# Spare matmuls and a new order in the boot of an RWKV-6 and tanh-shrink kernel

## The chip, the cores and the metric

The kernel runs on one core of one Trainium2 chip. The metric is the device time of one execution in microseconds (us). The engines are named as the profile names them: PE (matmuls), PEld (its weight loads), DVE (elementwise work), ACT (activations and copies), POOL, and SP, which mostly issues transfers.

## The reference

Two stages follow each other. The first is a recurrence over time for each of 4 batches and 8 heads; the second takes the result as 3072 rows of 384 columns.

```python
B, H, S, D = 4, 8, 768, 48
for t in range(S):
    cur = np.einsum('bhd,bhe->bhde', u[None] * kt, vt)
    y[:, :, t] = np.einsum('bhd,bhde->bhe', rt, state + cur)
    state = wt[:, :, :, None] * state + np.einsum('bhd,bhe->bhde', kt, vt)
# x: y as (3072, 384)
h = x @ w_in            # 384 -> 2048
g = h - np.tanh(h)
out = g @ w_out         # 2048 -> 384
```

## The kernel before, in words

**Blocks and tiles.** The work is cut into eight blocks, one for each batch and half of the sequence (384 tokens). A block needs its attention result `xT` (three tiles of 128 rows x 384 tokens), and then runs 16 tiles f0 to f15 of the second stage. In tile f, PE forms `hp` from `xT` and `w_in` (L703, six instructions), ACT moves it out as `h` (L706), DVE and ACT form `g` by a polynomial (`s`, `qa`, and the two products of L709), and two tiles later PE adds `g` times `w_out` into the three `acc` banks (L780). `hp` has one buffer, so hp of f+1 waits for h of f. From block 2 on a scheme with fewer products takes the place of L780.

**Attention.** The eight heads are four pairs; a half is two pairs (`HALVES`: pairs 2,3 first, then 0,1). A half has these steps, with a block's six chunks of 64 tokens:

- `behind` (a scan on DVE over the decays, with a small memset on POOL), `take_whole`, `before` (reciprocal and scan on DVE);
- `times_behind`, `times_before` (products with k and r on DVE), `times_u` (k scaled on ACT);
- `turn` (transposes on PE, copied to `ks` by ACT), `own` and `earlier` (scores within a chunk on PE, L434, put into the tile `scores` through a mask by DVE, L441);
- `update_1` (key-value products on PE, L482) and `update_2` (the states of the chunks, ten steps on DVE for block 0, L494 to L504);
- `from_scores` (L562) and `from_states` (L545), which add into two PSUM tiles `yp`, one for even and one for odd pairs; `result_out` copies them to `xT` and to `late` (pair 3), and `fill_holes` spreads `late` over the free rows of `xT` by six small transfers.

The two kinds of result matmuls are kept apart by a drain of PE and a wait on a semaphore (L578, L583), unless `more` says that the same kind goes on.

**The order.** PE, SP, DVE and ACT carry out their instructions in the order in which the code issues them. Block 0's attention is written out by hand in `boot` (L912), with nothing of the second stage to run beside it. For the others `plan(i)` (L869) says in which tile of the running block which step is issued: `phases` (steps with PE work) and `before` for the next block, `ahead` for the one after next, `loads` for transfers. A step's DVE part is issued behind that tile's own DVE operations.

**The weights.** They come as 64-bit numbers and are converted in the kernel: three ACT instructions (L249, L252, L253) and then two on DVE (L256, L257) for each tile f. `raw` has five buffers. Three loads are issued at the start; tiles 0 to 2 are converted in `boot`, tiles 3 to 15 in block 0's tiles. There the ACT part of conversion f+3 is issued in tile f and its DVE part in tile f+1, after s of f+1; so DVE's part of conversion 11 follows s of f9, and hp of f11 needs it.

**Scratch.** `boot` has four PSUM tiles of two banks in rotation (`scratch`); a new use waits for the last reader of the old one.

Of the kernel before, what the change touches and what calls it, by code (L numbers as in the profile page):

```python
# [41 lines left out]
BF16 = mybir.dt.bfloat16  # L42
# [8 lines left out]
B, H, S, D = 4, 8, 768, 48  # L51
P = 128
# [11 lines left out]
ALL = tuple(range(NPAIR))  # L64
# [55 lines left out]
def kernel(  # L120
# [12 lines left out]
    nc = tc.nc  # L133
# [26 lines left out]
    start = const.tile([P, UP * NCH * LP], F32, name="start", tag="start")  # L160
# [31 lines left out]
    ident = const.tile([P, P], F32, name="ident", tag="ident")  # L192
# [50 lines left out]
    def convert(f, raw, _, halves=False):  # L243


        lo, hi = raw[:, :, 0], raw[:, :, 1]
        a = w_sb[:, f, :].bitcast(I32)
        up = conv.tile([P, 2 * DM], I32, name="up", tag="up", bufs=4)
        nc.scalar.activation(out=a.bitcast(F32), in_=hi.bitcast(F32), func=AF.Copy, scale=HIGH_SCALE)  # L249
        low, high = (up.bitcast(t).rearrange("p (n two) -> p n two", two=2)[:, :, i]  # L250
                     for i, t in enumerate((U16, F16)))
        nc.scalar.activation(out=high, in_=hi.bitcast(F32), func=AF.Copy, scale=SIGN_SCALE)  # L252
        nc.scalar.activation(out=low, in_=lo.bitcast(U32), func=AF.Copy, scale=2.0 ** -29)  # L253

        def part(at):
            return [lambda: nc.vector.tensor_single_scalar(a[:, at], a[:, at], 3, op=ALU.logical_shift_left),  # L256
                    lambda: nc.vector.tensor_tensor(out=a[:, at], in0=a[:, at], in1=up[:, at], op=ALU.add)]  # L257

        if halves:
            return part(slice(0, DM)), part(slice(DM, 2 * DM))  # L260
        return part(slice(0, 2 * DM))

    def scratch(ps):
        return ps.tile([P, 2, BANK], F32, name="att", tag="att")

    fence, fences = tc.alloc_semaphore("fence"), []

    class Block:
# [177 lines left out]
        def own(self, ps, p0):  # L446
            return self.masked(ps, "k", "r", masks["diagonal"], p0)

        def earlier(self, ps, p0):
            return self.masked(ps, "post", "pre", masks["above"], p0)  # L450
# [132 lines left out]
                nc.tensor.drain().then_inc(fence, 1)  # L583
                fences.append(None)

        def result_out(self, pairs, apart=False, engines=(nc.scalar.copy,)):
            copies = []
            for p in reversed(pairs):
                n = p // 2
                src = self.yp[p % 2][:, :, n * NCP * L:(n + 1) * NCP * L].rearrange("e a (c t) -> e c a t", t=L)  # L590
                dst = self.xT[p] if p < KC else self.late
                dst = dst.rearrange("e (c a t) -> e c a t", a=2, t=L)
                for rows in (slice(0, D), slice(64, 64 + D)) if apart else (slice(0, P),):
                    copies.append(engines[p % len(engines)](out=dst[rows], in_=src[rows]))
            return copies[0]

        def fill_holes(self, engines):
# [102 lines left out]
    def first(xT, f, ps):  # L700
        hp = ps.tile([P, NB], F32, name="hp", tag="hp")
        for kc in reversed(range(KC)):
            nc.tensor.matmul(hp, lhsT=w_in_sb[:, f, kc, :], rhs=xT[kc],  # L703
                             start=(kc == KC - 1), stop=(kc == 0))
        h = dense.tile([P, NB], F32, name="h", tag="h")
        return h, nc.scalar.activation(out=h, in_=hp, func=AF.Copy, scale=1.0 / UPSCALE)  # L706
# [162 lines left out]
    def plan(i):  # L869


        converted = ()
        if i == 0:
            phases = {4: "turn", 6: "update", 8: "own", 11: "earlier", 13: "result 1"}
            before = {0: ("behind 0", "take_whole 0"), 1: ("times_behind 2",), 2: ("times_behind 0",),
                      3: ("before 2",), 4: ("times_u 2",), 5: ("before 0", "times_u 0"), 8: ("times_before", "held")}
            ahead = {14: ("behind 2", "take_whole 2"), 15: ("behind 0", "take_whole 0")}
            converted = range(READY, NF)
            loads = {f: "weights" for f in (0, 1, 3, 4, 5, 6, 7, 8, 9, 10)}
            loads.update({2: "v", 11: "w", 12: "k", 13: "r"})  # L880
        else:
            phases = {4: "earlier", 7: "turn", 10: "update", 12: "result 1"}
            if i == 1:
                before = {0: ("before 2",), 1: ("before 0",), 2: ("times_behind 2", "times_behind 0"),
                          3: ("times_before", "held")}
            else:
                before = {0: ("times_behind 2",), 1: ("times_behind 0",), 3: ("times_before", "held")}
            before.update({4: ("bound 2",), 5: ("product_u",), 6: ("bound 0", "product_r"), 7: ("product_sum",),
                           8: ("diagonal_in 2",), 9: ("diagonal_in 0",)})
            ahead = {10: ("behind 2", "take_whole 2"), 12: ("behind 0", "take_whole 0"), 13: ("before 2",),  # L890
                     15: ("before 0",)}
            loads = {1: "v", 3: "tokens k", 4: "tokens r", 7: "w", 9: "k", 11: "r"}
        return phases, before, ahead, converted, loads

    READY = 3
# [3 lines left out]
    raws = []  # L899
# [12 lines left out]
    def boot(ps, blk, later):  # L912
        h1, h2 = HALVES
        for p0 in HALVES:
            for name in ("w", "k", "r"):
                blk.load(name, p0, UP)
        blk.load_v()
        for _ in range(3):
            more_weights(nc.sync)
        ready = []  # L920

        def converted():
            for op in ready.pop(0):
                op()

        both = (h1, h1 + 1), (h2, h2 + 1)
        blk.behind(h1, UP)
        blk.take_whole(h1, UP)
        blk.before(h1, UP)
        blk.times_behind(h1, UP)  # L930
        blk.times_u(h1, UP)
        blk.turn(ps, h1)
        own = blk.own(ps, h1)
        blk.times_before(h1, UP)
        earlier = blk.earlier(ps, h1)
        blk.bound(h1)
        blk.bound(h2)
        blk.behind(h2, UP)
        blk.take_whole(h2, UP)
        blk.times_behind(h2, UP)  # L940
        blk.times_u(h2, UP)
        blk.turn(ps, h2)
        ins = blk.before(h2, UP)
        begin_behind(ins, later.load("w"))
        own()
        own = blk.own(ps, h2)
        blk.times_before(h2, UP)
        earlier()
        blk.update_1(ps)
        own()  # L950
        ready.append(convert(*raws.pop(0), halves=True))
        blk.results(ps)
        blk.result("from_scores", both[0])
        blk.update_2()
        ready.append(convert(*raws.pop(0)))
        later.bound(h1)
        blk.result("from_states", ALL, cs=(0, 1), more=True)
        earlier = blk.earlier(ps, h2)
        blk.result("from_states", ALL, cs=(2,))
        earlier()  # L960
        blk.result_out(both[0], True)
        later.bound(h2)
        blk.fill_holes([nc.sync, nc.scalar, nc.gpsimd])
        more_weights(nc.sync)
        blk.result("from_scores", both[1], True)
        for op in ready[0][0]:
            op()
        ins = blk.result_out(both[1], True, (nc.scalar.copy, nc.vector.tensor_copy))
        begin_behind(ins, more_weights(nc.sync))
        more_weights(nc.sync)  # L970
        later.load("k")
        later.load("r")
        nc.sync.dma_start(out=u_row, in_=u_all)
        blk.held(0, NPAIR)
        ready[0] = ready[0][1]
        converted()
        ready.append(convert(*raws.pop(0)))
        converted()
        later.prepare("behind 2")
        later.prepare("take_whole 2")  # L980
        converted()

    with tc.tile_pool(name="ps_boot", bufs=4, space=PSUM) as ps_boot:
        xT = blocks[0].begin()
# [4 lines left out]
    acc = [ps_d.tile([P, BANK], F32, name=f"acc{j}", tag=f"acc{j}") for j in range(NB // P)]  # L989
    count = const.tile([P, 1], F32, name="count", tag="count")  # L990
    ahead_of_h, rest, formed, extra, behind, due, summed = [], [], [], [], [], [], []
# [14 lines left out]
    for i, blk in enumerate(blocks):  # L1006
        here = xT
        later = blocks[i + 1] if i + 1 < len(blocks) else None
# [9 lines left out]
        phases, before, ahead, converted, loads = plan(i)  # L1018
# [3 lines left out]
        for f in range(NF):  # L1022
            now = i * NF + f
            for op in ahead_of_h:
                op()
            h, made = first(here, f, ps_d)
            g, ahead_of_h, square, later_ops = slight(h, now, i, f)
            for op in rest + behind + square + formed + extra:
                op()
            rest, behind, formed = later_ops, [], []  # L1030
# [41 lines left out]
            name, ins = loads.get(f), None  # L1072
            if name == "weights":
                ins = more_weights(nc.sync)
            elif name and name.startswith("tokens"):
                ins = later.load_tokens(name[-1]) if later else None
            elif name == "v":
                ins = later.load_v() if later else None
            elif name and after:
                ins = after.load(name)  # L1080
# [92 lines left out]
```

## Time and profile before

| what | value |
|---|---|
| median of 3 runs | 576.61 us (574.99 to 576.81) |
| profiled execution | 577.62 us |
| its span, first to last instruction | 575.8 us |
| busy in the span: PE, PEld, DVE, ACT, POOL | 552.6, 404.0, 486.9, 345.1, 10.9 us |
| mean granted clock of PE | 0.987 |
| hp of f0, f1, f2 of block 0 start | 28.70, 33.54, 38.33 us |
| hp of f11 of block 0 starts | 79.23 us |
| block 1's first hp starts | 104.02 us |

Each row of a timeline has its start in us from the start of the span, its length, the engine, the line of the kernel, the operation, what it writes and reads, the shape and the count. In brackets stands how long the engine had been idle before it, and what ended that idle time; "issue" means that the profile shows nothing that it waited for. In the page's slices each digit is a fortieth of the span (14.4 us) and the busy share in tenths; the row PEclk is the clock that PE was granted, in tenths of full speed.

### The profile page before, as it was taken

How to read it: one execution, taken by the hardware profiler on the slowest of the kernel's cores; microseconds unless marked ns; L12 is line 12 of the kernel's file. 1: busy time of each engine (PE TensorE's matmuls, PEld its weight loads, DVE VectorE, ACT ScalarE, POOL GpSimd, SP SyncE). 2: the span in 40 equal slices, each digit the busy share in tenths (PEclk: the TensorE clock that was granted, in tenths of full speed). 3: DMA queues.
4: the chain of work that ended last, by engine and by line, in shares of the span. 5: the costliest groups of instructions: out<-in, count | busy, mean ns of one | idle time of the engine just before them, and what ended most of it. 6: DMA issues, size and time to landing. Idle time of an engine off the chain costs nothing.

```text
span 575.8 us, 13873 instructions
## 1 busy us (share of the span) xinstructions
PE 552.6 (96%) x5644; PEld 404.0 (70%) x5644; DVE 486.9 (85%) x944; ACT 345.1 (60%) x702; POOL 10.9 (2%) x39
## 2 busy tenths in 40 slices
PE   3699999999999999999999999999999999999996
PEld 3546656566665787877877787778878777777763
DVE  8889996888879998889899988989998998668673
ACT  4889875333236765677565784667555775667441
POOL 6000000000000000000000000000000000000000
PEclk9869999999999999999999999999999999999999
DMA  8495553231302231032122222122321400100101
GB/s 313 133 390 188 173 176 121 72 95 57 111 12 84 83 111 59 10 95 87 56 67 83 84 85 84 52 61 76 102 62 47 125 1 3 40 14 1 43 1 44
DMA packets 32452, 50.38 MB, mean 88 GB/s; under 512 B 2560, under 2 KB 30336, under 8 KB 32384
## 3 DMA queue, kind: packets, MB, share of 16 engines
q1 hardware_dynamic: 32112, 49.36, 26.9%
q8 instruction: 45, 0.74, 0.5%
q14 instruction: 23, 0.19, 0.1%
q10 hardware_dynamic: 208, 0.05, 0.0%
q0 software_dynamic: 64, 0.05, 0.0%
HBM read 43.55 MB, written 4.72 MB: 84 GB/s over the span
## 4 chain that ended last, share of the span: by engine, by line
PE 86%; DVE 4%; ACT 4%; issue 1%; DVEq 0%
PE hp L703 40%; PE acc L818 21%; PE acc L780 10%; PE att L818 5%; PE att L545 2%; PE att L434 2%; PE att L562 2%; PE att L482 2%; PE att L457 1%; ACT up L252 1%; DVE w_sb L257 1%; ACT up L253 1%; ACT w_sb L249 1%; ACT h L706 1%; DVE sums L709 0%
## 5 line engine op out<-in xcount | busy, mean ns | idle before, releaser
L703 PE MATMUL hp<-xT,w_sb 128*128 128x384 f32 x768 | 274.2, 494 | 4.4 <-ACT h L706 2.4
L703 PEld LDWEIGHTS hp<-xT,w_sb 128*128 128x128 f32 x768 | 140.0, 193 | 86.7 <-ACT h L706 7.5
L706 ACT ACTIVATE h<-hp 128x384 f32<-128x384 f32 x128 | 62.9, 491 | 158.5 <-PE hp L703 156.9
L818 PE MATMUL acc<-forms,g 128*128 128x128 f32 x810 | 121.1, 277 | 0.5
L818 PEld LDWEIGHTS acc<-forms,g 128*128 128x128 f32 x810 | 108.7, 192 | 15.6 <-issue 1.2
L750 DVE TENSOR_TENSOR g<-g 128x256 f32<-128x256 f32 x225 | 95.4, 424 | 19.8 <-PE acc L818 0.9
L709 DVE SCALAR_TENSOR_TENSOR h<-h,s 128x384 f32<-128x384 f32 x128 | 70.3, 549 | 10.1 <-ACT s L724 9.6
L709 DVE SCALAR_TENSOR_TENSOR g<-qa,h 128x384 f32<-128x384 f32 x96 | 53.6, 558 | 17.5 <-PE acc L818 4.0
L780 PE MATMUL acc<-w_sb,sums 128*128 128x384 f32 x192 | 67.9, 490 | 0.2
L725 ACT ACTIVATE qa<-s,shift 128x384 f32<-128x384 f32 x90 | 55.4, 615 | 2.9
L727 ACT ACTIVATE junk<-s,shift 128x384 bf16<-128x384 f32 x90 | 53.9, 599 | 0.0
L780 PEld LDWEIGHTS acc<-w_sb,sums 128*128 128x128 f32 x192 | 35.7, 190 | 23.9 <-issue 0.5
L724 ACT ACTIVATE s<-h 128x384 f32<-128x384 f32 x90 | 47.1, 524 | 2.8
L818 PE MATMUL acc<-w_sb,g 128*128 128x128 f32 x270 | 44.9, 275 | 0.0
L818 PEld LDWEIGHTS acc<-w_sb,g 128*128 128x128 f32 x270 | 37.4, 192 | 0.0
L735 ACT ACTIVATE qa<-s,shift 128x384 f32<-128x384 f32 x38 | 23.5, 618 | 18.9 <-DVE top L732 18.9
L732 DVE CUSTOM_DVE_ANT_0 s<-h 128x384 f32<-128x384 f32 x38 | 21.1, 554 | 12.3 <-ACT h L706 12.3
L818 PE MATMUL att<-w_sb,g 128*128 128x128 f32 x180 | 30.2, 275 | 0.0
L818 PEld LDWEIGHTS att<-w_sb,g 128*128 128x128 f32 x180 | 26.4, 192 | 4.5
L363 DVE TENSOR_TENSOR_SCAN pre<-w,start 128x780 f32<-128x780 f32 x16 | 28.6, 1786 | 0.6
L374 DVE TENSOR_TENSOR_SCAN post<-w,seed 128x780 f32<-128x780 f32 x16 | 28.4, 1776 | 0.2 <-DMA w<-in_wT 0.2
L851 DVE TENSOR_TENSOR sums<-sums 128x256 f32<-128x256 f32 x72 | 27.8, 409 | 0.9
(84 smaller groups left out, 527.0 us busy)
## 6 DMA issues: line engine op xcount, KB each, us to landing
raw<-in_weights SPq DMA_DIRECT2D x16, 768.0 KB, 4.7
w<-in_wT SPq DMA_DIRECT2D x7, 780.0 KB, 4.6
k<-in_kT SPq DMA_DIRECT2D x7, 768.0 KB, 4.5
r<-in_rT SPq DMA_DIRECT2D x7, 768.0 KB, 4.5
v_sb<-in_v SPq DMA_DIRECT2D x8, 576.0 KB, 4.1
k<-in_tokens SPq DMA_DIRECT2D x6, 576.0 KB, 3.9
r<-in_tokens SPq DMA_DIRECT2D x6, 576.0 KB, 4.2
out_y<-sums SPq DMA_DIRECT2D x15, 128.0 KB, 1.9
```

The lines of the kernel that those rows point to most:

```text
L363: return nc.vector.tensor_tensor_scan(out=self.tile("pre")[:, cols], data0=self.tile("w")[:, cols], data1=start[:, 0:n * NCH * LP], initia ...
L374: return nc.vector.tensor_tensor_scan(out=back(t[:, 0:width]), data0=back(self.tile("w")[:, a:a + width]), data1=back(seed[:, 0:width]), i ...
L703: nc.tensor.matmul(hp, lhsT=w_in_sb[:, f, kc, :], rhs=xT[kc], start=(kc == KC - 1), stop=(kc == 0))
L706: return h, nc.scalar.activation(out=h, in_=hp, func=AF.Copy, scale=1.0 / UPSCALE)
L709: return lambda: nc.vector.scalar_tensor_tensor(out=out, in0=in0, scalar=scalar, in1=in1, op0=op0, op1=ALU.mult)
L724: nc.scalar.activation(out=s, in_=h, func=AF.Square)
L725: nc.scalar.activation(out=qa, in_=s, func=AF.Square, bias=shift[:, 4:5])
L727: nc.scalar.activation(out=junk[:, 0:NB], in_=s, func=AF.Relu, bias=shift[:, 5:6], accum_out=excess[:, at:at + 1])
L750: return lambda: nc.vector.tensor_tensor(out=G[:, to:to + 2], in0=two(G, g_at(q, a0), g_at(q, a1)), in1=two(G, g_at(q, b0), g_at(q, b1)), ...
L780: nc.tensor.matmul(acc, lhsT=g[:, j * P:(j + 1) * P], rhs=w_out_sb[:, f, :], start=(f == self.first), stop=(f == NF - 1))
L818: nc.tensor.matmul(to, lhsT=G[:, g_at(q, a), :], rhs=rhs, start=start, stop=stop, skip_group_check=True)
L851: nc.vector.tensor_tensor(out=at[0], in0=at[1], in1=at[2], op=OPS[op])
```

## The change

- A helper `busy(to, n)` issues n matmuls of 128 rows and 512 columns in bf16 on the identity tile, whose result nothing reads. In `boot` three stand between `from_states` of chunks 0,1 and of chunks 2, and seven behind the latter, into a scratch tile; in block 0 two stand ahead of hp in f1 and in f2, into `acc[0]`.
- In `boot` the `earlier` scores of pairs 0,1 are formed and masked ahead of `update_1`. `from_scores` runs for all four pairs at once, then `from_states` of chunks 0,1, and at last `from_states` of chunks 2. The conversion of tile 2 is issued on ACT before that last part. The two `bound` steps of block 1 come after the result copies.
- The result copies all follow the last matmuls: ACT takes pairs 3 and 1 (one `yp` tile), DVE pairs 2 and 0 (the other). Before, ACT took 3, 2 and 0, and DVE took 1; pairs 3 and 2 were copied ahead of `from_scores` of pairs 0,1. The DVE parts of the three conversions follow the copies.
- `behind 2` and `take_whole 2` of block 1 move from `boot` to f0 of block 0, and `behind 0` of block 1 from f0 to f1.
- `behind 2` and `behind 0` of block 2 move from f14 and f15 of block 0 to f0 and f1 of block 1. In block 1 `before 2` and `before 0` go from f0 and f1 to f2 and f3, the two `times_behind` from f2 to f2 and f3, `times_before` from f3 to f4, `earlier` from f4 to f6, `turn` from f7 to f8, and the two loads of tokens from f3 and f4 to f4 and f5.

```diff
+    def busy(to, n):
+        by = ident.bitcast(BF16)
+        for _ in range(n):
+            nc.tensor.matmul(to, lhsT=by[:, 0:P], rhs=by.unsqueeze(1).to_broadcast([P, 2, 2 * P]), start=True,
+                             stop=True, skip_group_check=True)
...
-        def result_out(self, pairs, apart=False, engines=(nc.scalar.copy,)):
+        def result_out(self, pairs, copy=None):
...
-                for rows in (slice(0, D), slice(64, 64 + D)) if apart else (slice(0, P),):
-                    copies.append(engines[p % len(engines)](out=dst[rows], in_=src[rows]))
+                for rows in (slice(0, D), slice(64, 64 + D)) if copy else (slice(0, P),):
+                    copies.append((copy or nc.scalar.copy)(out=dst[rows], in_=src[rows]))
...
-            before = {0: ("behind 0", "take_whole 0"), 1: ("times_behind 2",), 2: ("times_behind 0",),
-                      3: ("before 2",), 4: ("times_u 2",), 5: ("before 0", "times_u 0"), 8: ("times_before", "held")}
-            ahead = {14: ("behind 2", "take_whole 2"), 15: ("behind 0", "take_whole 0")}
+            before = {0: ("behind 2", "take_whole 2"), 1: ("behind 0", "take_whole 0", "times_behind 2"),
+                      2: ("times_behind 0",), 3: ("before 2",), 4: ("times_u 2",), 5: ("before 0", "times_u 0"),
+                      8: ("times_before", "held")}
+            ahead = {}
...
             if i == 1:
-                before = {0: ("before 2",), 1: ("before 0",), 2: ("times_behind 2", "times_behind 0"),
-                          3: ("times_before", "held")}
+                phases = {6: "earlier", 8: "turn", 10: "update", 12: "result 1"}
+                before.update({0: ("behind 2", "take_whole 2"), 1: ("behind 0", "take_whole 0"),
+                               2: ("before 2", "times_behind 2"), 3: ("before 0", "times_behind 0"),
+                               4: ("times_before", "held", "bound 2")})
...
-            loads = {1: "v", 3: "tokens k", 4: "tokens r", 7: "w", 9: "k", 11: "r"}
+            loads = {1: "v", 3 + (i == 1): "tokens k", 4 + (i == 1): "tokens r", 7: "w", 9: "k", 11: "r"}
...
+        earlier = blk.earlier(ps, h2)
+        own()
         blk.update_1(ps)
-        own()
         ready.append(convert(*raws.pop(0), halves=True))
+        earlier()
         blk.results(ps)
-        blk.result("from_scores", both[0])
+        blk.result("from_scores", ALL)
         blk.update_2()
         ready.append(convert(*raws.pop(0)))
-        later.bound(h1)
         blk.result("from_states", ALL, cs=(0, 1), more=True)
-        earlier = blk.earlier(ps, h2)
-        blk.result("from_states", ALL, cs=(2,))
-        earlier()
-        blk.result_out(both[0], True)
-        later.bound(h2)
+        idle = scratch(ps)[:, 0]
+        busy(idle, 3)
+        ready.append(convert(*raws.pop(0)))
+        blk.result("from_states", ALL, True, cs=(2,))
+        busy(idle, 7)
+        blk.result_out((3,), nc.scalar.copy)
         blk.fill_holes([nc.sync, nc.scalar, nc.gpsimd])
         more_weights(nc.sync)
-        blk.result("from_scores", both[1], True)
-        for op in ready[0][0]:
-            op()
-        ins = blk.result_out(both[1], True, (nc.scalar.copy, nc.vector.tensor_copy))
+        blk.result_out((1,), nc.scalar.copy)
+        blk.result_out((2,), nc.vector.tensor_copy)
+        ins = blk.result_out((0,), nc.vector.tensor_copy)
         begin_behind(ins, more_weights(nc.sync))
...
+        later.bound(h1)
+        later.bound(h2)
+        for op in ready[0][0] + ready[0][1] + ready[1] + ready[2]:
+            op()
         blk.held(0, NPAIR)
-        ready[0] = ready[0][1]
-        converted()
-        ready.append(convert(*raws.pop(0)))
-        converted()
-        later.prepare("behind 2")
-        later.prepare("take_whole 2")
-        converted()
...
+            if i == 0 and f in (1, 2):
+                busy(acc[0], 2)
```

More of the change, by code (lines that the diff above doesn't have):

```diff
@@ L882, in plan @@
             phases = {4: "earlier", 7: "turn", 10: "update", 12: "result 1"}
+            before = {0: ("times_behind 2",), 1: ("times_behind 0",), 3: ("times_before", "held"), 4: ("bound 2",),
+                      5: ("product_u",), 6: ("bound 0", "product_r"), 7: ("product_sum",), 8: ("diagonal_in 2",),
+                      9: ("diagonal_in 0",)}
             if i == 1:
-                before = {0: ("before 2",), 1: ("before 0",), 2: ("times_behind 2", "times_behind 0"),
-                          3: ("times_before", "held")}
[L886 to L889, printed above, removed]
+                phases = {6: "earlier", 8: "turn", 10: "update", 12: "result 1"}
+                before.update({0: ("behind 2", "take_whole 2"), 1: ("behind 0", "take_whole 0"),
+                               2: ("before 2", "times_behind 2"), 3: ("before 0", "times_behind 0"),
+                               4: ("times_before", "held", "bound 2")})
             ahead = {10: ("behind 2", "take_whole 2"), 12: ("behind 0", "take_whole 0"), 13: ("before 2",),
                      15: ("before 0",)}
-            loads = {1: "v", 3: "tokens k", 4: "tokens r", 7: "w", 9: "k", 11: "r"}
+            loads = {1: "v", 3 + (i == 1): "tokens k", 4 + (i == 1): "tokens r", 7: "w", 9: "k", 11: "r"}
         return phases, before, ahead, converted, loads
@@ L920, in boot @@
         ready = []
-        def converted():
-            for op in ready.pop(0):
-                op()
-        both = (h1, h1 + 1), (h2, h2 + 1)
         blk.behind(h1, UP)
@@ L948, in boot @@
         earlier()
+        earlier = blk.earlier(ps, h2)
+        own()
         blk.update_1(ps)
-        own()
         ready.append(convert(*raws.pop(0), halves=True))
+        earlier()
         blk.results(ps)
-        blk.result("from_scores", both[0])
+        blk.result("from_scores", ALL)
         blk.update_2()
         ready.append(convert(*raws.pop(0)))
-        later.bound(h1)
         blk.result("from_states", ALL, cs=(0, 1), more=True)
-        earlier = blk.earlier(ps, h2)
-        blk.result("from_states", ALL, cs=(2,))
-        earlier()
-        blk.result_out(both[0], True)
-        later.bound(h2)
+        idle = scratch(ps)[:, 0]
[4 more added lines that the diff above has]
+        blk.result_out((3,), nc.scalar.copy)
         blk.fill_holes([nc.sync, nc.scalar, nc.gpsimd])
         more_weights(nc.sync)
-        blk.result("from_scores", both[1], True)
-        for op in ready[0][0]:
-            op()
-        ins = blk.result_out(both[1], True, (nc.scalar.copy, nc.vector.tensor_copy))
+        blk.result_out((1,), nc.scalar.copy)
+        blk.result_out((2,), nc.vector.tensor_copy)
+        ins = blk.result_out((0,), nc.vector.tensor_copy)
         begin_behind(ins, more_weights(nc.sync))
```

## The prediction, made before the result was known

> **What bounds the kernel now.** I read the page's slices first, then the PE timeline, then DVE's, then the busy table by stretches. The slices (14.4 us each) show PE near full from the third on, and a granted clock that dips only in the second and third.
>
> ```profile
> PE   3699999999999999999999999999999999999996
> DVE  8889996888879998889899988989998998668673
> PEclk9869999999999999999999999999999999999999
> ```
>
> In the PE timeline (start, length, instruction, and in brackets the idle time ahead of it with its releaser) PE has gaps in the boot and in the first two tiles, then runs without a gap from 38.33 to 78.07, waits once, and runs on through blocks 1 and 2.
>
> ```profile
> 18.89 0.62 PE L482 MATMUL att<-v_sb,ks 64*64 64x48 f32 x28 [0.45 <-issue]
> ...
> 22.91 0.43 PE L545 MATMUL att<-pre,states 48*48 48x64 f32 x15 [1.67 <-issue]
> ...
> 28.70 4.21 PE L703 MATMUL hp<-xT,w_sb 128*128 128x384 f32 x6 [1.05 <-ACT xT L594]
> 33.54 4.21 PE L703 MATMUL hp<-xT,w_sb 128*128 128x384 f32 x6 [0.63 <-ACT h L706]
> 38.33 2.20 PE L703 MATMUL hp<-xT,w_sb 128*128 128x384 f32 x6 [0.58 <-ACT h L706]
> ...
> 79.23 1.21 PE L703 MATMUL hp<-xT,w_sb 128*128 128x384 f32 x3 [1.00 <-DVE w_sb L257]
> ```
>
> The one wait, at 79.23, is tile f11 of block 0. It waits for the conversion of its weights on DVE, and from there to the end PE sets the time. So what counts is **when DVE finishes conversion 11**. DVE's timeline:
>
> ```profile
> 22.49 0.35 DVE L504 TENSOR_TENSOR states<-states,att 128x192 f32<-128x192 f32 x1
> 24.11 1.01 DVE L441 COPY_PREDICATED scores<-mask_all,att 128x768 f32<-128x768 uint8 x1 [1.27 <-PE att L434]
> ...
> 26.60 1.14 DVE L594 COPY xT<-att 48x384 f32<-48x384 f32 x2 [0.55 <-ACT xT L594]
> ...
> 33.66 0.55 DVE L732 CUSTOM_DVE_ANT_0 s<-h 128x384 f32<-128x384 f32 x1
> ...
> 38.31 0.56 DVE L732 CUSTOM_DVE_ANT_0 s<-h 128x384 f32<-128x384 f32 x1 [1.06 <-ACT h L706]
> ```
>
> Idle there: 1.27, 0.55, 1.06, and 0.70 at 53.7 (waiting for qa). Nothing else until conversion 11 ends at 79.08: 3.58 us of idle in 60 us. The rest is work in program order. An earlier PE cannot gain more than this idle.
>
> The table by stretches (length, then busy PE, PEld, DVE, ACT, POOL, granted clock, DMA share, GB/s) gives the clock. It was 1.00 to 24.68, 0.50 to 38.33, and 1.00 after.
>
> ```profile
> 17.85:24.68 6.83, 4.43 (x252) 3.88 (x248) 5.18 (x13) 4.74 (x8) 0.13 (x2) 1.00 0.26 93
> 24.68:31.50 6.82, 4.78 (x53) 3.06 (x54) 6.00 (x11) 6.53 (x11) 1.11 (x2) 0.50 0.57 187
> 31.50:38.33 6.83, 5.62 (x10) 2.12 (x8) 5.45 (x11) 4.15 (x7) 0.00 (x0) 0.50 1.03 395
> ```
>
> A stretch with PE busy 65% ended in the fall, one with 70% did not lift the clock, one with 82% did.
>
> **What the Trainium skill says.** "TensorE: Matmul & The Clock Gate", Part 1: the clock is halved by default, activity over a free-running window releases it, idleness takes it back. The trace agrees on the two values; its changes lie 6.83 and 13.65 us apart. The same page, "Back-to-back issue gap", prices a 512-column bf16 matmul at 427 ns at half clock and 216 ns at full clock; no such matmul is in the trace. "Runtime: NRT & Kernel Launch", "Instruction fetch mechanics": instructions come in blocks of 256 and crossing into one is mostly hidden. Here it is not hidden in the boot. The two gaps marked "issue" (0.45 and 1.67 us) stand before PE's 449th and 705th records, 256 apart, with no semaphore wait; 16 KB instruction transfers of the trace end 1.6 and 1.4 us before each gap ends. "PSUM — Partial Sum Buffer", "Specifications (TRN2)": ACT and DVE may read different banks at once at full rate. Before, their result copies hardly overlap (ACT to 26.51, DVE 26.60 to 27.74, ACT from 27.69).
>
> **The change part by part.**
>
> *1. Scores ahead of states.* Own's matmuls for pairs 0,1 end at 16.89. The off-diagonal ones now follow at once, but need times_before (DVE, 16.26 + 0.95 = 17.21): 48 instructions, about 1.3 us with the clock still low to 17.85, end 18.5. update_1's 96 instructions at 22 ns (28 in 0.62) end at 20.7, crossing record 449 about when it was available before (18.89). On DVE the masked copy (0.9) now stands ahead of update_2, and update_2 needs update_1's first 64 instructions: start about 20.25 instead of 18.92, ten operations 3.92 as before, end 24.17.
>
> *2. PE to the last result matmul.* from_scores for all pairs, 96 x 18.5 ns (47 in 0.85 plus pipeline), meets record 705 half way, which cannot be there before 22.9 (blocks came 18.89 to 22.91, 4.02 apart, and nothing in the change brings that transfer forward). It ends at 23.8; from_states of chunks 0,1 (64 instructions, 1.2) at 25.1; three spare matmuls 0.65, 25.75. The 32 of chunks 2 cross record 961 after some 11; one more block interval gives 26.9, and 21 x 18.5 ns give **27.3**. Bounds: 24.9 if the blocks cost nothing, 27.8 at half clock.
>
> *3. Copies and holes.* All eight half copies now come after 27.3. DVE does pairs 2 and 0: 4 x 0.57 = 2.28 instead of 1.14, so **+1.14 us of DVE work**, idle from 24.17 to 27.5 (3.3 us), end 29.8. ACT does pair 3 (0.97, to 28.5), then issues two hole transfers (0.63 + 0.86 before) with pair 1 queued behind them: done about 31.0. The holes land 1.9 after issue, 30.5; before they were hidden behind from_scores. f0's w_in conversion on DVE now comes after the copies: 29.8 + 0.9 = 30.7. So hp f0 starts at about 31.05 against 28.70.
>
> *4. The seven spare matmuls* (1.5 us at full clock, 3.0 at half) lie in 27.3 to 31.05, where PE waits: nothing. Those at f1 and f2, two each, 0.43 to 0.85, lie in the waits for h (0.63, 0.58 before): nothing at full clock, at most 0.3 each at half.
>
> *5. ACT and queues.* Conversion 2 (2.8) moves from 28.67 into ACT's idle time at 21.5; the two bounds (1.1 each) go after pair 1's copy, 31.0 to 33.2, just hidden behind hp f0 (h at 33.3). SP's hole transfers wait for the late tile, 28.5 instead of 25.5, and three weight loads, k, r and u_row queue behind them: all 3 us later. k, landing 9.3 after issue, comes at about 41, times_behind wants it at 42.3; weight load 3 may hold ACT by up to 1 us. I take nothing for both.
>
> *6. DVE from the copies to f11.* Three conversions 1.74 + 1.46 + 1.50 = 4.7, held 0.1: s of f0 at 34.6 instead of 33.66. From there before had 45.42 to conversion 11, less idle 1.06 and 0.70 = 43.66. The first scan of block 1 moves from the boot into f0: +1.9 (30.19 to 32.09). So 34.6 + 45.56 = 80.16, plus some 0.25 of new idle = 80.4; f11 starts at 80.55 against 79.23: **+1.3**, if the clock holds.
>
> *7. The clock.* In 17.85 to 24.68 PE would now be busy about 5.4 of 6.83 (79%): it holds. In 24.68 to 31.5: 1.3 + 0.4 + 1.5 + 0.45 = 3.6 (53%), under the 65% that ended in a fall. The spare matmuls run out some 2 us ahead of hp f0. With a fall at 31.5 hp f0 ends 1.2 later (s of f0 35.0, idle 0.4) and hp f1 runs 35.0 to 38.85: s of f1 at 39.35 where DVE is ready at 38.5, idle 0.85. Sum about **+2.2**. Wholly at half clock: f0 35.25, f1 40.1, s at 40.65, +3.5.
>
> *8. Two scans to block 1.* In f14 and f15 of block 0 PE never waited for DVE: no gain. In block 1, f0 to f4 get behind 2, behind 0 and later neighbours: DVE per tile 3.6, 3.6, 4.56, 4.56, 4.6 against PE's 3.87, a lag of up to 1.9 us, paid back by f8, where diagonal work is light and turn's PE time comes. acc waits for sums with 3.7 us to spare; qa ahead of h leaves 0.9. Nothing; at most 1 us if that slack is overestimated. Key tokens issued a tile later land about when product_u asks: 0 to 0.2, inside the same slack.
>
> The sum on the profiled execution (575.79 span + 1.83 around it = 577.62) is +2.2, its own clock phase assumed. That execution stands 1.01 above the median; I carry the difference over: 576.61 + 2.2 = **578.8**.
>
> **Rivals.** *Clock kept* through f0 and f1 by another window phase: +1.3, 577.9. *Clock wholly lost*: +3.5, 580.1. *The other side:* the instruction stream does not pace the boot, because the transfers start earlier in the new order. Then from_states ends at 24.9 (23.8 for the last state, plus the spare three and 0.6), everything from step 3 on comes 2.4 to 2.6 earlier, f11 at 77.95: -1.3, 575.3. It decides from an end below 26.0, where conversion 11 equals 79.08. For it: the three spare matmuls fit the wait for the last state exactly in that case. Against it: two gaps 256 records apart. The floor for any gain is all idle gone: 3.58 - 1.14 = 2.4, 574.2.
>
> **How the numbers follow.** About 0.3% (1.7 us) is what a measurement can tell from no change. Forecast case 0.38 (slower 0.32, same 0.06); clock kept 0.25 (same 0.17, slower 0.08); wholly lost 0.13 (slower); not paced 0.19 (same 0.12, faster 0.07); towards the floor 0.05 (faster). Faster 0.12, same 0.35, slower 0.53. The range leaves out part of the last case and of the third: 575.0 to 580.3.
>
> **What would show it.** Right: an "issue" gap in from_scores near 22 and one in the last from_states near 26.5; update_2 starting near 20.3; DVE idle about 3 us before its first copy at 27.5; hp f0 near 31; f11 near 80.5 to 81.5 with a wait for L257; no DVE wait of PE in block 1. Wrong: from_states ending before 26, DVE reaching s of f0 before 33, f11 before 79, or PE waiting in block 1.

## The result, and the profile after

| | before | after |
|---|---|---|
| median of 18 runs each | 575.86 us (574.9 to 578.1) | 578.04 us (577.26 to 578.9) |
| ratio after to before | | 1.0035, 95% interval 1.0025 to 1.0044 |
| profiled execution | 577.62 us | 577.93 us |
| its span, mean granted clock | 575.8 us, 0.987 | 576.2 us, 1.000 |

The changed kernel is slower by 0.35%, 2.2 us between the medians. The two profiled executions are only 0.3 us apart. That gap between 2.2 and 0.3 is a finding of its own: the first profiled execution of the kernel before was one of its dear (slower) ones, as the run before_again shows.

The slices of the page after (each digit 14.4 us) show no dip of the granted clock; before it dipped in the second and third.

```profile
PE   3679999999999999999999999999999999999996
...
DVE  8799996699879998889999899989998998668673
...
PEclk9999999999999999999999999999999999999999
```

PE's timeline after has the gaps marked "issue" again, now in update_1, in from_scores and in the last from_states; the spare matmuls (L270); the waits ahead of f0 and f2; and the wait for conversion 11.

```profile
18.83 1.38 PE L489 MATMUL att<-v_sb,ks 64*64 64x48 f32 x80 [0.25 <-issue]
...
22.59 0.89 PE L569 MATMUL att<-scores,v_sb 64*48 64x64 f32 x48 [1.53 <-issue]
...
26.15 0.54 PE L552 MATMUL att<-pre,states 48*48 48x64 f32 x19 [0.32 <-issue]
26.62 1.68 PE L270 MATMUL att<-ident 128*128 128x512 bf16 x7
30.29 2.20 PE L711 MATMUL hp<-xT,w_sb 128*128 128x384 f32 x6 [1.99 <-DVE w_sb L256]
32.33 0.59 PE L270 MATMUL acc<-ident 128*128 128x512 bf16 x2
33.07 2.20 PE L711 MATMUL hp<-xT,w_sb 128*128 128x384 f32 x6
35.11 0.59 PE L270 MATMUL acc<-ident 128*128 128x512 bf16 x2
37.28 2.20 PE L711 MATMUL hp<-xT,w_sb 128*128 128x384 f32 x6 [1.58 <-ACT h L714]
...
79.82 2.17 PE L711 MATMUL hp<-xT,w_sb 128*128 128x384 f32 x6 [1.34 <-DVE w_sb L257]
```

hp of f0 and f1 take 2.20 us instead of 4.21, but f0 starts at 30.29 instead of 28.70. f11 starts at 79.82 instead of 79.23, still with a wait for DVE (1.34), which is the only wait of PE for another engine from there to the end of block 1. From f11 to the end of the span both kernels need the same: 496.6 before, 496.4 after. DVE's timeline:

```profile
20.02 0.33 DVE L501 TENSOR_TENSOR states<-att,whole 128x192 f32<-128x192 f32 x1
...
26.64 2.28 DVE L602 COPY xT<-att 48x384 f32<-48x384 f32 x4 [2.71 <-PE att L552]
...
34.01 0.55 DVE L740 CUSTOM_DVE_ANT_0 s<-h 128x384 f32<-128x384 f32 x1
...
37.52 0.55 DVE L740 CUSTOM_DVE_ANT_0 s<-h 128x384 f32<-128x384 f32 x1
...
39.46 1.77 DVE L381 TENSOR_TENSOR_SCAN post<-w,seed 128x780 f32<-128x780 f32 x1
...
78.71 0.96 DVE L257 CUSTOM_DVE_ANT_0 w_sb<-w_sb,up 128x1536 uint16<-128x1536 uint16 x1
```

update_2 starts at 20.02, DVE then waits 2.71 for the last result matmuls, makes four copies instead of two, and comes to s of f0 at 34.01. The scan at 39.46 now lies behind s of f1. From the first copy at 26.64 to the end of conversion 11 at 79.67 DVE's timeline shows no wait at all. ACT's timeline shows what stands ahead of hp of f0: pair 3's copy, two hole transfers, and only then pair 1's copy; later conversion 3 waits for its weights.

```profile
26.72 0.97 ACT L602 COPY late<-att 48x384 f32<-48x384 f32 x2 [3.06 <-PE att L552]
27.72 1.51 ACTq L609 DMA_DIRECT2D xT<-late  x2
29.28 0.96 ACT L602 COPY xT<-att 48x384 f32<-48x384 f32 x2 [1.59 <-issue]
...
33.62 0.92 ACT L249 ACTIVATE w_sb<-raw 128x768 f32<-128x768 f32 x1 [0.60 <-DMA raw<-in_weights]
```

For the wait of hp of f0 the profile names DVE's L256. But f0's `w_in` was converted by 30.01 and pair 1's copy ended at 30.24, and in the run conv_first below, where the conversions come earlier, hp of f0 does not move. So it is the copies and hole transfers that hold it.

The table by stretches, cut at the same times as before, has PE busy 72%, 66% and 75%, and the clock at 1.00 in all three.

```profile
17.85:24.68 6.83, 4.92 (x282) 4.35 (x273) 5.60 (x13) 5.81 (x7) 0.13 (x2) 1.00 0.27 97
24.68:31.50 6.82, 4.52 (x50) 2.27 (x47) 4.45 (x10) 3.10 (x7) 1.11 (x2) 1.00 0.25 66
31.50:38.33 6.83, 5.10 (x17) 2.37 (x16) 6.55 (x13) 6.07 (x10) 0.00 (x0) 1.00 1.01 400
```

### The profile page after: what moved, and what is told of

Its sections match the earlier page's. It is cut to its first block, busy times and chain, and to the rows that moved or that the text cites. A ratio compares the mean times of both kernels' runs of the same rounds, so it can differ in the third digit from the quotient of the medians.

```text
span 576.2 us, 13901 instructions
## 1 busy us (share of the span) xinstructions
PE 550.1 (95%) x5658; PEld 401.1 (70%) x5658; DVE 487.7 (85%) x946; ACT 344.4 (60%) x700; POOL 10.0 (2%) x39
## 4 chain that ended last, share of the span: by engine, by line
PE 86%; DVE 10%; issue 1%; DMA 1%; ACT 0%; PEld 0%; SPq 0%; DVEq 0%; PEldq 0%
PE hp L711 40%; PE acc L826 21%; PE acc L788 10%; PE att L826 5%; PE att L552 2%; PE att L441 2%; PE att L569 2%; DVE w_sb L257 2%; PE att L489 2%; PE att L464 1%; DMA r<-in_rT 1%; DVE scores L448 1%; DVE post L381 1%; DVE sums L717 1%; DVE w_sb L256 1%
## 5 line engine op out<-in xcount | busy, mean ns | idle before, releaser
L711 PE MATMUL hp<-xT,w_sb 128*128 128x384 f32 x768 | 270.3, 488 | 6.4 <-ACT h L714 2.9
L711 PEld LDWEIGHTS hp<-xT,w_sb 128*128 128x128 f32 x768 | 138.3, 190 | 86.8 <-ACT h L714 7.8
## 6 DMA issues: line engine op xcount, KB each, us to landing
v_sb<-in_v SPq DMA_DIRECT2D x8, 576.0 KB, 3.9
k<-in_tokens SPq DMA_DIRECT2D x6, 576.0 KB, 3.9
r<-in_tokens SPq DMA_DIRECT2D x6, 576.0 KB, 4.5
```

## The experiments

Theory A at the start: the boot now ends later, DVE has idle time there and two copies more, and DVE's conversion 11 passes that on to f11. Each comparison is with runs of the kernel before made beside it on the same chip; their medians were 576.09 us (beside before_again, no_spare, conv_first, plan_only), 576.05 (conv_and_scan, before_spare, after_later_product, before_later_product) and 576.26 (scans_moved, records_shifted, conv_scan_k).

**The kernel before once more** (before_again). No edit.

> The kernel before, unchanged, for a second trace and for its spread. Theory A (DVE's conversion 11 sets the start of f11, and the first profiled execution was a dear one because the granted clock fell to half for 13.65 us over f0 and f1): executions whose mean granted clock is near 1.0 take 575.0 to 575.6 us, those at 0.987 take 576.5 to 577.6; ratio 1.000. In a trace without the fall hp of f0 to f1 takes 2.1 instead of 4.2, DVE's wait of 1.06 at s of f1 is gone and f11 starts at 77.2 to 78.2 instead of 79.23. Rival (the clock is of no account, the spread has another cause): times do not follow the granted clock.

Measured: 575.55 us, ratio 0.9995 (0.9984 to 1.0005). Its profiled execution took 575.17 at a clock of 0.999. PE's timeline there:

```profile
28.15 2.20 PE L703 MATMUL hp<-xT,w_sb 128*128 128x384 f32 x6 [1.22 <-ACT xT L594]
31.48 2.20 PE L703 MATMUL hp<-xT,w_sb 128*128 128x384 f32 x6 [1.13 <-ACT h L706]
35.14 2.20 PE L703 MATMUL hp<-xT,w_sb 128*128 128x384 f32 x6 [1.46 <-ACT h L706]
```

```profile
76.74 2.17 PE L703 MATMUL hp<-xT,w_sb 128*128 128x384 f32 x6 [1.32 <-DVE w_sb L257]
```

f0 and f1 ran in 2.20 each, and f11 started at 76.74, half a microsecond earlier than I expected. The spread follows the clock: over the 126 runs of the kernel before in the experiments (these 13 and the 113 beside them), those with a mean granted clock under 0.9875 have a median of 577.43, up to 0.9915 of 576.84, up to 0.9955 of 575.60, and above that of 575.17. So theory A's part on the spread holds. Like for like, with the clock kept in both, the change moves f11 from 76.74 to 79.82 and the span from 573.4 to 576.2: **+3.1 and +2.8 us**. Runs say the same: above a mean clock of 0.9955 the medians are 575.17 before (15 runs) and 577.94 after (14 runs). The medians of all runs are nearer to each other because the kernel before often pays for the clock and the changed one seldom does (0.991 to 1.000 in its 18 runs).

**Only the scans of block 2 moved** (plan_only).

```diff
-            ahead = {14: ("behind 2", "take_whole 2"), 15: ("behind 0", "take_whole 0")}
+            ahead = {}
...
+                before.update({0: ("behind 2", "take_whole 2"), 1: ("behind 0", "take_whole 0"),
...
```

> The kernel before with only the two scans of block 2 moved to block 1, with the later places of the steps behind them; boot and block 0's first tiles as before. Theory A (DVE has slack there): ratio to before 1.000, within 0.1%, and no wait of PE for DVE in block 1. Rival (the fuller DVE in block 1 is what makes the change slower): 1.5 to 2.2 us over before, with PE waits for DVE between f2 and f8 of block 1.

Measured: 575.88 us, ratio 0.9997 (0.9988 to 1.0006), and no wait of PE for DVE in block 1. This part costs and gains nothing. Its profiled execution also shows that not every fall of the clock is paid for: the clock was at half from 27.40 to 30.81, so hp of f0 took 3.65, but f11 started at 76.57 and the execution took 574.70, one of the shortest.

```profile
27.86 3.65 PE L703 MATMUL hp<-xT,w_sb 128*128 128x384 f32 x6 [1.48 <-ACT xT L594]
```

**All moves of scans, with spare matmuls, in the old boot** (scans_moved).

```diff
...
-        later.prepare("behind 2")
-        later.prepare("take_whole 2")
...
+            before = {0: ("behind 2", "take_whole 2"), 1: ("behind 0", "take_whole 0", "times_behind 2"),
...
```

> The kernel before with the spare matmuls of before_spare and all of the change's moves of scans: behind 2 of block 1 from the boot into f0 of block 0, behind 0 to f1, the two scans of block 2 to block 1. The boot's order and copies stay as before. Theory A (the order of the boot and its late copies are what the change costs; a scan that goes from ahead of s of f0 to behind it leaves DVE's sum to conversion 11 the same): 575.2 to 575.6, ratio to before 0.998 to 1.000. Rival (the scan moved into f0 and f1 costs its 1.9 us): 577.0 to 577.4.

Measured: 575.76 us, 0.16 over theory A's range, ratio 0.9992 (0.9982 to 1.0003). Against before_spare below (0.9984, 0.9973 to 0.9995) that is at most a small loss; the intervals overlap. Its profiled execution kept the clock and spans 573.9 us. Most of the 2.8 us, some 2.3 by the spans (573.9 to 576.2), must then come from the boot's new order and its copies.

**The change without spare matmuls** (no_spare): the three calls of `busy` left out.

> The changed kernel without its 14 spare matmuls. Theory A (they hold the clock, but the three in the boot stand 0.65 us ahead of the last result matmuls): the last from_states ends 0.5 to 0.7 earlier; where the clock still holds, the time is 577.4, where it falls, 578.5 to 579.5; on the median 577.4 to 578.7, with a wider spread than the changed kernel's 1.6. Rival (the spare matmuls are what makes the change slower): 576.0 or less, as before. Rival (they are needed): over 579.

Measured: 580.69 us, ratio 1.0071 (1.0056 to 1.0087). A miss for theory A, which took the spare matmuls for nearly neutral: in this order they are needed. PE's timeline:

```profile
25.82 0.44 PE L552 MATMUL att<-pre,states 48*48 48x64 f32 x16 [1.49 <-issue]
29.93 4.21 PE L711 MATMUL hp<-xT,w_sb 128*128 128x384 f32 x6 [3.66 <-ACT xT L602]
34.71 4.21 PE L711 MATMUL hp<-xT,w_sb 128*128 128x384 f32 x6 [0.58 <-ACT h L714]
```

The last from_states does end earlier (26.26 against 26.69), as expected. But PE then has nothing to do for 3.66 us, the clock goes to half from 28.88 to 39.12, hp of f0 and f1 take 4.21 each, and f11 starts at 81.79. In the new order the spare matmuls give back 0.36% (1.0071 to 1.0035); without them the rest of the change costs about 0.7%.

**Spare matmuls alone, in the kernel before** (before_spare).

```diff
...
         blk.result("from_states", ALL, cs=(2,))
+        idle = scratch(ps)[:, 0]
+        busy(idle, 3)
...
         blk.result("from_scores", both[1], True)
+        busy(idle, 5)
...
+            if i == 0 and f in (1, 2):
+                busy(acc[0], 2)
```

> The kernel before with spare matmuls alone: three behind the last from_states, five behind the last from_scores, two each ahead of hp of f1 and f2, all in waits of 0.4 to 1.5 us that its second trace shows. Theory A: they hold the clock through f0 and f1, so that the dear executions (576.5 to 577.6) go and the median comes to 575.2 to 575.5, ratio 0.998 to 1.000. Rival (they hold up the work behind them): hp of f0 later than 28.15 and a median over 576.0.

Measured: 575.27 us, ratio 0.9984 (0.9973 to 0.9995); 21 of its 22 runs lie between 574.37 and 576.41, with mean clocks of 0.997 to 1.000; of the 57 runs of the kernel before beside it 7 reach 0.997. Theory A's numbers are met: this part of the change is a small gain when taken alone. The dear executions are rarer, not gone: its profiled one took 577.23 at 0.995, with the clock at half from 23.30 to 26.71. But the clock is not all of that execution: the load of k came late there too, in the old order of the boot, and DVE waited for it, so that f11 started at 78.96.

```profile
40.55 0.96 DVE L395 TENSOR_TENSOR post<-k,post 128x768 f32<-128x768 f32 x1 [0.89 <-DMA k<-in_kT]
```

**DVE's conversions ahead of the copies** (conv_first).

```diff
+        for op in ready[0][0] + ready[0][1] + ready[1]:
+            op()
         blk.result_out((3,), nc.scalar.copy)
...
-        for op in ready[0][0] + ready[0][1] + ready[1] + ready[2]:
+        for op in ready[2]:
             op()
```

> The changed kernel with the DVE parts of conversions 0 and 1 issued ahead of the result copies instead of behind them, so that they fill DVE's idle time of 2.7 us there. Theory A (idle DVE time in the boot is what the change costs): s of f0 goes to about 33.0, held up by hp f0, and f11 from 79.82 to about 78.75: 577.0, 0.2% under the changed kernel. Rival (PE's later start of f0 is what costs): f0 stays at 30.2 to 30.3 and the time stays 578.0.

Measured: 578.02 us, ratio 1.0034, the same as the change. Theory A missed here as well. DVE's timeline:

```profile
33.17 0.56 DVE L740 CUSTOM_DVE_ANT_0 s<-h 128x384 f32<-128x384 f32 x1 [1.79 <-ACT h L714]
...
37.00 0.56 DVE L717 SCALAR_TENSOR_TENSOR sums<-qa,h 128x384 f32<-128x384 f32 x1 [0.90 <-ACT qa L743]
37.47 0.55 DVE L740 CUSTOM_DVE_ANT_0 s<-h 128x384 f32<-128x384 f32 x1
```

DVE's idle time was not saved but moved: 1.79 us of waiting for h of f0 and 0.90 for qa, and s of f1 stands at 37.47 as in the changed kernel (37.52). So up to s of f1 there are **two chains** of nearly the same length. One is DVE's work. The other is the last result matmul, pair 3's copy, the hole transfers and pair 1's copy behind them, hp of f0 at 30.4, h, conversion 3 on ACT, qa, h of f1. Here the profile names the hole transfers themselves:

```profile
30.43 2.17 PE L711 MATMUL hp<-xT,w_sb 128*128 128x384 f32 x6 [2.03 <-DMA xT<-late]
```

To shorten DVE's chain alone in this stretch brought nothing. No run shortened the other one alone.

**The scan back in the boot as well** (conv_and_scan).

```diff
+        later.prepare("behind 2")
+        later.prepare("take_whole 2")
...
-            before = {0: ("behind 2", "take_whole 2"), 1: ("behind 0", "take_whole 0", "times_behind 2"),
+            before = {0: ("behind 0", "take_whole 0"), 1: ("times_behind 2",),
```

> The changed kernel with DVE's conversions 0 and 1 ahead of the result copies, and the first scan of block 1 (behind 2, take_whole 2) back in the boot, behind conversion 2; behind 0 back in f0. Theory A: in the run with the conversions alone ahead DVE waited 1.79 us for h of f0 and 0.90 for qa, and s of f1 stayed at 37.47; now the scan (1.9) fills that wait, s of f1 stays where ACT lets it, at 37.5, and from there DVE has 40.2 us to conversion 11, as before, instead of 42.1: f11 at 77.8, 576.0 us, 0.3% under the changed kernel and level with the kernel before. Rival (the late start of hp of f0, not DVE's work, sets f11): 578.0.

Measured: 577.47 us, ratio 1.0022 (1.0013 to 1.0031): better than the change, and not the 576.0 of theory A. In its profiled execution f11 started at 79.43 and not at 77.8: the clock was at half from 31.55 to 34.97, inside hp of f0, and DVE waited for what comes late:

```profile
34.54 0.56 DVE L740 CUSTOM_DVE_ANT_0 s<-h 128x384 f32<-128x384 f32 x1 [0.51 <-ACT h L714]
...
40.95 0.96 DVE L395 TENSOR_TENSOR post<-k,post 128x768 f32<-128x768 f32 x1 [0.79 <-DMA k<-in_kT]
```

k is the load that SP's queue issues behind the hole transfers and three weight loads, at 30.70 (28.49 in the first profile of the kernel before); it landed some 3 us later than there. The fall is not all that theory A missed: the four runs with a mean clock of 1.000 took 576.93 to 577.35.

**k ahead of two weight loads** (conv_scan_k).

```diff
-        begin_behind(ins, more_weights(nc.sync))
+        begin_behind(ins, later.load("k"))
         more_weights(nc.sync)
-        later.load("k")
+        more_weights(nc.sync)
```

> The kernel conv_and_scan with the load of k ahead of two of the three weight loads on SP's queue. In conv_and_scan DVE waited 0.79 us for k at times_behind, since the queue starts 3 us later than before. Theory A: that wait goes, f11 0.5 to 0.8 earlier, 576.7 to 577.0 us. Rival (the delayed weight loads then hold ACT up instead): 577.5 or more.

Measured: 578.61 us, ratio 1.0042. The rival was right: DVE's wait for k is gone, and ACT now waits for the weights of conversion 4.

```profile
39.39 0.92 ACT L249 ACTIVATE w_sb<-raw 128x768 f32<-128x768 f32 x1 [0.95 <-DMA raw<-in_weights]
```

In both orders tried, with the queue 2 to 3 us later than before, one of its users waits.

**The records shifted** (records_shifted).

```diff
+        for _ in range(4):
+            pre = scratch(ps)
+        few_cols = shift.bitcast(BF16)[:, 0:4]
+        for _ in range(60):
+            nc.tensor.matmul(pre[0:4, 0, 0:4], lhsT=few_cols, rhs=few_cols, start=True, stop=True,
+                             skip_group_check=True)
         blk.behind(h1, UP)
```

> The changed kernel with 60 matmuls of 4 columns (two records each) at the head of the boot, where PE has nothing to do until 9.6 us. Theory A (PE's instructions come in blocks of 256 records, some 4 us apart in the boot): the gaps without a releaser stay at the records 449, 705 and 961 counted from the start, and so fall on other work, 120 records earlier in it: none or next to none in the wait for times_before, one near the end of update_1 (till about 21.2), one in from_states of chunks 0,1 (till about 25.1); the last from_states ends near 27.3 instead of 26.7 and the time is 578.0 to 578.8. Rival (the gaps belong to the work, not to the count): gaps in the same matmuls as in the changed kernel, 578.0.

Measured: 580.08 us in 4 runs, ratio 1.008. The spare work ends at 2.75, long before PE has anything to do, and the gap moves with the count:

```profile
1.11 1.64 PE L936 MATMUL att<-shift 128*4 128x4 bf16 x60 [1.11 <-DVE shift L145]
...
18.24 1.39 PE L489 MATMUL att<-v_sb,ks 64*64 64x48 f32 x81
21.64 0.38 PE L489 MATMUL att<-v_sb,ks 64*64 64x48 f32 x10 [2.00 <-issue]
```

The gap of 2.00 stands before record 705 once more (records are counted in the order of the program, a matmul and its weight load each; the trace lacks some seven of those ahead of each gap), now in update_1 (L489) and not in from_scores; from_scores has none. That of record 449 fell into the wait for times_before, as expected; I saw none at 961, where PE came later. The last from_states ended at 27.67, expected 27.3. The gaps belong to the count. The time came out 1.3 to 2.1 over the expectation; the clock was at half for two stretches of 3.41 us in its profiled execution (22.12 and 32.36), and hp of f0 took 3.21.

**times_before of block 1 behind conversion 11**, in the changed kernel (after_later_product) and in the kernel before with spare matmuls (before_later_product).

```diff
-                      8: ("times_before", "held")}
+                      9: ("times_before", "held")}
```

> The changed kernel with block 1's times_before (1.85 us of DVE) in f9 of block 0 instead of f8, that is behind conversion 11 and not ahead of it. Theory A (conversion 11 on DVE sets f11): PE's wait of 1.34 us at f11 goes, f11 at 78.4 to 78.5, 576.6 to 576.8 us. Rival (something on PE or ACT sets it, the wait only looks like DVE's): no change, 578.0.

Measured: 576.54 us, ratio 1.0004 (0.9993 to 1.0015), 0.3% under the change and just better than theory A's range. PE's timeline at f11:

```profile
75.98 2.10 PE L788 MATMUL acc<-w_sb,sums 128*128 128x384 f32 x6
77.91 2.10 PE L711 MATMUL hp<-xT,w_sb 128*128 128x384 f32 x6
```

No wait is left there; f11 starts at 77.91, although the clock was at half from 31.20 to 34.62. So DVE's conversion 11 did set f11.

> The kernel before with the spare matmuls of the run before_spare and with block 1's times_before in f9 instead of f8. Theory A: the wait of 1.32 us at f11 that the second trace of the kernel before shows goes as well; f11 at 75.4, 574.0 to 574.4 us, ratio 0.996 to 0.998. Rival (PE has no slack ahead of f11): 575.4.

Measured: 574.42 us, ratio 0.9965 (0.9951 to 0.9978), at the upper end of theory A's range. f11 starts without a wait, at 76.44 and not at 75.4, in an execution whose clock was at half from 23.12 to 26.54.

```profile
76.44 2.10 PE L710 MATMUL hp<-xT,w_sb 128*128 128x384 f32 x6
```

This version is faster than the kernel before by 0.35%, and the changed kernel is slower than it.

## Why the prediction was right, and where it was not

**The sign and the mechanism were right**: the copies come late, DVE's conversion 11 ends late, and f11 waits for it (scans_moved, after_later_product). **The size came out by luck**: +2.2 us forecast, +2.18 measured on the medians, 578.8 and 578.04. The sum of 2.2 compares two profiled executions that both have a fall of the clock. Between the two that were profiled the difference is 0.31. The other 1.87 is that the first profiled execution stood 1.76 above its kernel's median of 18 runs, and the one after 0.11 below its own. Two errors cancelled.

*Step 1*: update_2 at 20.02 (20.25 forecast). The prediction says both that the clock was at 1.00 up to 24.68 and, in this step, that it was low up to 17.85. The pace of the matmuls speaks for the second: 48 score products took 1.56 us from 15.33 before, and 0.93 from 17.27 after. *Step 2*: gaps at the records 449, 705 and 961, in the matmuls named; the last from_states ended at 26.69 instead of 27.3, because record 705 came at 22.59 and not 22.9, and record 961 came 3.56 us after it and not 4.0. This rules out the rival "not paced": its point was an end below 26.0. *Step 3*: copies from 26.64 to 28.92 on DVE (27.5 to 29.8), pair 1 done at 30.24 (31.0), hp of f0 at 30.29 (31.05): all early by 0.8 to 0.9. ACT's and DVE's copies ran at once, each at its length of before (ACT 0.97 for two; DVE 2.28 for four, 1.14 for two before). *Step 4*: the seven spare matmuls took 1.68 (1.5 forecast), ended at 28.30, and PE waited 1.99 more; they cost nothing, as said, and the pairs at f1 and f2 neither. *Step 6*: from s of f0 to the end of conversion 11 DVE took 45.66 (45.56 forecast). *Step 8*: nothing, shown by plan_only.

*Step 5* was too easy. Conversion 3 waited 0.60 for its weights, and k was late enough to matter in conv_and_scan (0.79). SP's hole transfers started 2.2 us later than before (27.72), not 3. In the changed kernel itself none of this reached f11, since DVE ran without a wait from 26.64 on.

*Step 7 failed.* I forecast a fall of the clock at 31.5 from a busy share of PE of 53% in 24.68 to 31.5, against the 65% that had ended in a fall before. The share was 66% and the clock held. But the rule itself does not hold: in before_again PE was busy 61% and then 52% in these two stretches, and the clock stayed at 1.00.

```profile
17.85:24.68 6.83, 4.15 (x224) 3.61 (x224) 5.54 (x14) 5.06 (x9) 0.13 (x2) 1.00 0.26 91
24.68:31.50 6.82, 3.58 (x55) 1.99 (x55) 6.31 (x13) 6.65 (x12) 1.11 (x2) 1.00 0.65 217
```

The Trainium skill ("TensorE: Matmul & The Clock Gate", Part 1) says the window is free-running; the runs agree, as the edges lie elsewhere in each execution (a fall at 24.68, 28.88 or 31.55). Shares taken over one execution's edges do not carry to the next. Cut at each execution's own edges, every 3.41 us from its first change of the clock, the picture is clearer. These are the changed kernel (no fall), conv_and_scan (a fall at 31.55) and no_spare (a fall at 28.88), in this order:

```profile
26.69:30.10 3.41, 1.61 (x7) 0.53 (x7) 3.18 (x7) 1.76 (x4) 1.11 (x2) 1.00 0.17 42
28.14:31.55 3.41, 0.92 (x4) 0.65 (x4) 3.18 (x7) 2.32 (x5) 0.33 (x1) 1.00 0.55 150
25.47:28.88 3.41, 0.44 (x16) 0.29 (x16) 2.49 (x5) 0.95 (x2) 1.11 (x2) 1.00 0.07 15
```

The changed kernel's seven spare matmuls fell into one such stretch (47%) and the clock held. In conv_and_scan the same seven had run out at 28.18, just as the stretch began (27%), and it fell. So in these executions it hung on where the edges lay. The case "clock kept" was the one that the changed kernel's profiled execution met: its +1.3 against the first profiled execution, of which +0.59 at f11 was measured, 0.7 less for step 3's reason.

*The carry-over failed too.* I added the difference to the median as if the kernel before always had the fall. It has it in part of its runs only; like for like the change costs 2.8 at a kept clock, and the spared falls give back some 0.6 on the median. The kernel before gains when its clock holds: f11 at 76.74 instead of 79.23. The sum charged the change against a base that was 2.5 us dearer there.

**Open**: how the loss divides between the late hole transfers, the two more DVE copies, and SP's late queue. The runs show that the two chains up to s of f1 are nearly as long as each other, and that no single one of the edits tried frees more than 0.3%. I also did not try the old copies behind the new order of the matmuls.

## What to carry to other kernels

A spare matmul in a wait of PE is nearly free and can hold the clock for the work behind it (0.16% here, alone), but it must be taken without an order that lengthens the wait. In this kernel the hole transfers and a copy were hidden behind the last matmuls; to gather all matmuls first and copy at the end laid both bare. Look at which work of the slower engine stands ahead of the one operation that the bound engine waits for: to put 1.85 us of DVE work behind it brought 0.2 to 0.3%, by moving one step of the plan to the next tile, while the whole change lost 0.35%. When the clock differs from execution to execution, compare profiled executions of like clock before you carry a difference over to a median.

## What the runs showed of the hardware

PE's instruction blocks of 256 records can set the pace where matmuls are small: the kernel before and the changed one have gaps of 0.25 to 1.67 us before the records 449 and 705, the changed one also of 0.32 before 961, and the shifted one has 2.00 before 705; the blocks come 3.5 to 4.0 us apart. The gaps follow the count (records_shifted). That they wait for the instructions themselves fits the 16 KB instruction transfers, which end 1.3 to 1.6 us before each gap does in these kernels, but no run changed those transfers. The Trainium skill ("Runtime: NRT & Kernel Launch", "Instruction fetch mechanics") calls such a crossing mostly hidden; in this boot it is not. The clock changed after multiples of 3.41 us: it was at half for 13.65, 10.24 or 3.41 us in different executions. Cut at their own edges, the ten falls in the boot and the first tiles of these profiles each follow a stretch of 3.41 us in which PE was busy 13 to 60%. Every stretch of 42% or less was followed by a fall; of those from 47 to 60% three were and seven were not. So the busy share alone does not decide it in that range, and the runs leave open what does.
